# Backward attention loop: operand loads in 28 pieces and result stores issued by SP between the transposing transfers

## The chip, the core and the metric

The kernel runs on one core of a Trainium2 chip. The metric is the device time of one execution in microseconds (us). The core has five engines that this text names: PE (matrix products), DVE (elementwise work on two operands), ACT (functions and copies), POOL (elementwise work, and an issuer of transfers through a software queue) and SP (which only issues transfers, through a hardware queue). All transfers run on the core's 16 DMA engines. Matmuls read SBUF and write PSUM; DMA moves data between SBUF and HBM, and can transpose two-byte data on its way.

## The reference

A transformer block with adaptive layer norm: attention with 32 heads of 16 columns over 2048 tokens of width 512, then a two-layer MLP with a squared ReLU, each with a modulated layer norm and a gate. The kernel computes the block's output and the gradients of nine inputs for a given output gradient.

```
h = layernorm(x) * (1 + ca) + sa
x = x + ga * attention(h, wqkv, wo)
h = layernorm(x) * (1 + cb) + sb
x = x + gb * (relu(h @ w1 + b1)**2 @ w2 + b2)
out, vjp = jax.vjp(block, ...);  grads = vjp(grad_out)
```

The part that matters here is the backward pass of attention. For each head, with E = exp(scores) and the row factors folded into the operands:

```
dS = E * (dO' V'^T)          # 2048 x 2048 per head, elementwise product
dV = E^T dO'    dK = dS^T Q'    dQ = dS K
```

## The kernel before

The kernel runs in phases: layer norm and projections; a forward loop of attention with the MLP's work woven in; weight gradients (lines 776 to 838); the backward loop of attention (lines 840 to 987); and a last phase (from line 989) that turns dQ, dK and dV into the gradients of `x` and `wqkv`.

The backward loop has 1024 steps. `steps` lists them as (head group, key chunk, query tile, pair): 8 head groups of four heads, 4 key chunks of 512 keys (`kc4`), 16 query tiles of 128 queries (`qt`), 2 pairs of heads (`pr`). A head group is 128 steps, a key chunk of it is 32 steps (`BLK`), and 8 steps form a group (`GRP`) of four query tiles.

In each step PE forms scores (`emit_S`, line 852, one step ahead) into a PSUM tile, ACT takes their exponential into `E_u` (line 856), PE forms dO V^T (`emit_D`, line 864), and DVE multiplies the two into `dS_u` (line 870). PE then adds to `accVK`, which holds dV and dK of the key chunk (`emit_V`, line 906, and `emit_K`, line 914). For dQ, dS has to stand with the keys on the partitions. So after the second pair of a query tile SP issues a transposing transfer of `dS_u` into `dST` (line 876): 128 x 2048 elements for the first three tiles of a group and 128 x 1024 for the fourth, whose other half PE transposes (`emit_T`, line 894) and ACT copies (`emit_C`, line 898). `emit_Q` (line 935) multiplies `dST` with K, ten to seventeen steps after the group's first step; ACT copies the result out, and POOL adds it into `dQacc` (line 948) or, in the last key chunk, into `dQstage` (line 953).

`dS_u` has five buffers, one for each two steps, so a buffer is written again ten steps later, and only when its transposing transfer and PE have read it. `dST` has three buffers, one per group.

Two kinds of plain transfers run beside this, all issued by POOL. The operands of the next head group are loaded by `load_one`, nineteen loads, one each five steps from step 32 of a head group on: sixteen of 17 rows of 2048 elements (`iq`, `ik`, `ido`, `iv`, four heads each, 68 KB, line 771) and three of 128 x 2048 elements (`sdo`, `sq`, `sk`, 512 KB, line 767). The tiles have two copies, one per parity of the head group. The results are stored by `put_rows` (line 884): when a head group's dV and dK are copied into `dVKstage`, eight stores of 16 rows of 2048 elements, and when its dQ is complete, four more from `dQstage`. In the last head group the stores are made by pieces of 512 columns, as soon as each is ready, 48 in all. The last phase reads them back from `dT_st` into `dqT` (line 998).

The order of instructions on an engine is the order of the program, loosened by a scheduler; `chain` ties instructions of one queue into a fixed order, here PE's matmuls, and POOL's transfers and sums. SP's transposing transfers are not chained before. Each transfer issued by SP waits until the one eight places before it in SP's queue has landed, since they share eight completion counters; POOL's queue has eight of its own.

Of the kernel before, what the change touches and what calls it, by code (L numbers as in the profile page):

```python
# [17 lines left out]
BF = dt.bfloat16  # L18
F32 = dt.float32

P = 128
# [3 lines left out]
DH = 16  # L25
HG = 8
# [7 lines left out]
def kernel(  # L34
# [8 lines left out]
    TT = n // P  # L43
    QC = n // 512
# [10 lines left out]
    POOL = nc.gpsimd  # L55
    SP = nc.sync
# [34 lines left out]
    def issue_order(later, earlier):  # L91
        tc.add_manual_dep(later.ins, earlier.ins.name, order_only, reason="issue order on one engine")
# [7 lines left out]
    qp_st = dram.tile([HG, P, TT, P], BF, name="qp_st")  # L100
    kp_st = dram.tile([HG, P, TT, P], BF, name="kp_st")
    dop_st = dram.tile([HG, P, TT, P], BF, name="dop_st")
# [7 lines left out]
    dT_st = dram.tile([3, D, n], BF, name="dT_st")  # L110
# [82 lines left out]
    with ExitStack() as ph:  # L193
# [20 lines left out]
        for ic in range(DC):  # L214
            for t in range(3):
                src = wqkv_nat[:, ic, t * 512:(t + 1) * 512].rearrange("p (hg h d) -> p hg h d", hg=HG, h=4)
# [13 lines left out]
        for t in range(TT):  # L230
            for which in range(3):
# [4 lines left out]
                if which < 2:  # L236
                    pad = tokpad[which][t % 2]
                    c0 = DH if which == 0 else 0
# [7 lines left out]
                    else:  # L246
# [3 lines left out]
                                 in_=pad[:])  # L250
# [54 lines left out]
    with ExitStack() as ph:  # L305
# [19 lines left out]
        def chain(key, x):  # L325
            if key in last:
                issue_order(x, last[key])
            last[key] = x

        def pe(mm):  # L330
            chain("pe", mm)
# [236 lines left out]
        with ExitStack() as pa_:  # L568
# [50 lines left out]
            def emit_S(u):  # L619
                qc, hg, kt = units[u]  # L620
                kt_sb, qt_sb, _ = loads[u // TT]
                pair_ps = (sbank[0], sbank[1 + u % 2])
                ET_t[u] = fe.tile([P, 4, 512], BF, name="ET", tag="ET")
                for hq in range(4):
                    r = 32 * hq
                    pe(PE.matmul(pair_ps[hq // 2][:, hq % 2, :], kt_sb[r:r + 32, kt * P:(kt + 1) * P],  # L626
                                 qt_sb[r:r + 32, :], start=True, stop=True, tile_position=(r, 0)))
                for pair in range(2):
                    ACT.activation(ET_t[u][:, 2 * pair:2 * pair + 2, :], pair_ps[pair][:], AF.Exp, scale=SCALE)  # L629
# [108 lines left out]
    strm = tc.alloc_tile_pool(name="phIs", bufs=2, side="right")  # L738
# [5 lines left out]
    steps = [(hg, kc4, qt, pr) for hg in range(HG) for kc4 in range(QC) for qt in range(TT) for pr in range(2)]  # L744
    NS = len(steps)
    BLK = 2 * TT
# [10 lines left out]

    loads = {}
    LOADS = [(nm, src, j) for nm, src in (("iq", QtP), ("ik", KtP), ("ido", dOtP), ("iv", VtP)) for j in range(4)]
    LOADS += [("sdo", dop_st, None), ("sq", qp_st, None), ("sk", kp_st, None)]  # L760

    def load_one(hg, i):
        nm, src, j = LOADS[i]
        L = loads.setdefault(hg, {})
        if j is None:
            L[nm] = strm.tile([P, TT, P], BF, name=nm, tag=nm)
            chain("pool", POOL.dma_start(out=L[nm][:], in_=src[hg]))
        else:
            L[nm] = ops[nm][hg % 2]
            r = 32 * j  # L770
            chain("pool", POOL.dma_start(out=L[nm][r:r + DH + 1, :], in_=src[hg][r:r + DH + 1, :]))

    for i in range(len(LOADS)):
        load_one(0, i)
# [60 lines left out]
    with ExitStack() as ph:  # L835
# [8 lines left out]
        E_t, dS_t, dS_q, dST_t, acc_t = {}, {}, {}, {}, {}  # L844
# [13 lines left out]
        def emit_D(s):  # L858
            hg, kc4, qt, pr = steps[s]
            L = loads[hg]  # L860
            ps = psu.tile([P, 2, 512], F32, name="psD_u", tag="pu")
            for hi in range(2):
                r = 32 * (2 * pr + hi)
                pe(PE.matmul(ps[:, hi, :], L["ido"][r:r + 32, qt * P:(qt + 1) * P],  # L864
                             L["iv"][r:r + 32, kc4 * 512:(kc4 + 1) * 512],
                             start=True, stop=True, tile_position=(r, 0)))
            if pr == 0:
                dS_q[s // 2] = ework.tile([P, 4, 512], BF, name="dS_u", tag="dS_u", bufs=5)
            dS_t[s] = dS_q[s // 2][:, 2 * pr:2 * pr + 2, :]
            DVE.tensor_tensor(dS_t[s], ps[:], E_t[s][:], ALU.mult)  # L870
            g = s // GRP
            if s % GRP == 0:
                dST_t[g] = tpool.tile([P, 4, 16, P], BF, name="dST", tag="dST")
            if pr == 1:
                nb = 16 if qt % 4 < 3 else 8
                SP.dma_start(out=dST_t[g][:, qt % 4, 0:nb, :],
                             in_=dS_q[s // 2].rearrange("q h k -> q (h k)")[:, 0:nb * P], transpose=True)

        stage = {}

        def put_rows(st, hg, c0, w, parts):
            for t3, off in parts:
                for hq in range(4):
                    chain("pool", POOL.dma_start(
                        out=dT_st[t3, hg * 64 + hq * DH:hg * 64 + (hq + 1) * DH, c0:c0 + w],
                        in_=st[32 * hq + off:32 * hq + off + DH, c0:c0 + w]))

        def emit_T(g, half):
            if half == 0:
# [12 lines left out]
        def emit_V(s):  # L902
            hg, kc4, qt, pr = steps[s]
            for hi in range(2):
                r = 32 * (2 * pr + hi)
                pe(PE.matmul(accVK[r:r + 32, :], loads[hg]["sdo"][:, qt, r:r + 32], E_t[s][:, hi, :],  # L906
                             start=(qt == 0), stop=False, tile_position=(0, r), skip_group_check=True))
            del E_t[s]
# [18 lines left out]
        def emit_Q(g, kt):  # L927
            hg, kc4, qt, _ = steps[g * GRP]
            L = loads[hg]
            if kt == 0:  # L930
                acc_t[g] = psa.tile([P, 512], F32, name="accQ", tag="pq")
            accQ = acc_t[g]
            for hq in range(4):
                r = 32 * hq
                pe(PE.matmul(accQ[r:r + 32, :], L["sk"][:, kc4 * 4 + kt, r:r + 32],  # L935
                             dST_t[g][:, :, hq * 4 + kt, :],
                             start=(kt == 0), stop=(kt == 3), tile_position=(0, r), skip_group_check=True))
            if kt == 3:
                del dST_t[g], acc_t[g]
                qc = qt // 4  # L940
                sl = slice(qc * 512, (qc + 1) * 512)
                if kc4 == 0:
                    ACT.activation(dQacc[:, sl], accQ[:], AF.Identity)
                else:
                    part = wk.tile([P, 512], F32, name="dQpart", tag="dQpart")
                    ACT.activation(part[:], accQ[:], AF.Identity)  # L946
                    if kc4 < QC - 1:
                        chain("pool", POOL.tensor_tensor(dQacc[:, sl], part[:], dQacc[:, sl], ALU.add))  # L948
                    else:
                        if qc == 0:  # L950
                            stage["q"] = stg.tile([P, n], BF, name="dQstage", tag="dQstage")
                        st = stage["q"]
                        chain("pool", POOL.tensor_tensor(st[:, sl], part[:], dQacc[:, sl], ALU.add))
                        if hg == HG - 1:
                            put_rows(st, hg, qc * 512, 512, ((0, 0),))
                        elif qc == QC - 1:
                            put_rows(st, hg, 0, n, ((0, 0),))

        emit_S(0)
        for s in range(NS + 12):  # L960
            r = s % (BLK * QC) - BLK
            if s < NS and r >= 0 and r % 5 == 0 and r // 5 < len(LOADS) and steps[s][0] + 1 < HG:
                load_one(steps[s][0] + 1, r // 5)
            if s + 1 < NS:
                emit_S(s + 1)
            if s < NS:
                emit_D(s)
            v = s - 1
            if 0 <= v < NS:
                if v % BLK == 0 and v > 0:  # L970
                    pass
                elif v % BLK == 1 and v > 1:
                    emit_V(v - 1)
                    emit_V(v)
                else:
                    emit_V(v)
            if 0 <= s - 2 < NS:
                emit_K(s - 2)
            g, j = divmod(s - GRP - 2, GRP)
            if 0 <= g < NS // GRP:  # L980
                if 1 <= j <= 2:
                    emit_T(g, j - 1)
                if 1 <= j <= 4:
                    emit_C(g, j - 1)
                for kt in ((0,), (1,), (2, 3))[j - 5] if j >= 5 else ():
                    emit_Q(g, kt)

    strm.release()
    with ExitStack() as ph:
# [6 lines left out]
        for jb in range(12):  # L996
            t3, b = divmod(jb, 4)
# [92 lines left out]
    if _rest_zero:  # L1090
        zt = persist.tile([P, 2048], BF, name="zeros2048")
        DVE.memset(zt[:], 0.0)
        for o in _rest_zero:
# [9 lines left out]
            while r0 < R:  # L1103
                rr = min(P, R - r0)
                c0 = 0
# [35 lines left out]
```

## Time and profile before

| what | value |
|---|---|
| time, median of 3 runs (range) | 2865.84 us (2865.42 to 2877.51) |
| the profiled execution's own time | 2866.86 us |
| its span | 2865.1 us |
| backward loop, first to last `dS_u` multiply | 1363.1 to 2729.9 us |
| PE busy | 2295.4 us (80%) |
| ACT busy | 2256.1 us (79%) |
| DVE busy | 1853.7 us (65%) |
| POOL busy | 579.0 us (20%) |
| hardware queue q1 (SP): packets, share of 16 engines | 1239268, 61.8% |
| software queue q0 (POOL): packets, share of 16 engines | 32704, 12.6% |
| one transposing transfer: issue on SP, from issue to landing (medians) | 1.629 us, 3.9 us |

The span is what the profiler saw of one execution, from the first instruction to the last. The page gives busy times per engine, a chain of waits followed back from the end, groups of instructions by line with what ended the idle time before them, and the transfers by queue. `q1` is the queue that SP feeds, `q0` the one that POOL feeds, `q10` that of ACT. A line such as `L870 DVE ... x1024 | 1218.5, 1221 | 150.1 <-PE psD_u L864 99.5` reads: 1024 instructions of line 870 on DVE, busy 1218.5 us in all, 1221 ns each, DVE idle 150.1 us just before them, 99.5 us of it ended by the matmul of line 864.

### The profile page before, as it was taken

To read this page: it belongs to the slowest core of one execution; us is meant where nothing else is said; L and a number is where in the kernel's file an instruction comes from. 1 tells how busy PE (TensorE), PEld (TensorE's weight loads), DVE (VectorE), ACT (ScalarE), POOL (GpSimd) and SP (SyncE) were. 2 spreads that over 40 slices of the span, in tenths; PEclk is the share of its full clock that TensorE was granted. 3 is DMA by queue.
4 is the path that set the end of the run, shared out by engine and by line. 5 is a ranking of instruction groups with operands and counts; after the bars stand their busy time and mean duration, and the time that the engine had idled before them with its cause. 6 is when DMAs were issued, how large, how long until landed. Compare 5 with 4: busy or idle time off the path is not lost.

```text
span 2865.1 us, 48307 instructions
## 1 busy us (share of the span) xinstructions
PE 2295.4 (80%) x18156; PEld 783.1 (27%) x18261; DVE 1853.7 (65%) x2432; ACT 2256.1 (79%) x2854; POOL 579.0 (20%) x766
## 2 busy tenths in 40 slices
PE   4788879778877875748888888888888888888868
PEld 2323223222322321314222222222222222222223
DVE  5433344425524452743898989989899898989934
ACT  3799999999999995010898989989899898989812
POOL 7311100410230041052012121111212111121221
PEclk8989969878987996969799999999999998999989
DMA  7931245435553544667799999999989999999985
GB/s 200 221 101 62 70 145 122 132 115 116 128 146 87 134 112 138 151 172 233 156 193 202 186 203 194 190 195 189 204 188 199 193 187 196 189 189 188 184 229 132
DMA packets 1275073, 470.61 MB, mean 164 GB/s; under 512 B 1219635, under 2 KB 1244342, under 8 KB 1273046
## 3 DMA queue, kind: packets, MB, share of 16 engines
q1 hardware_dynamic: 1239268, 357.49, 61.8%
q0 software_dynamic: 32704, 105.82, 12.6%
q10 hardware_dynamic: 2866, 4.20, 0.4%
q8 instruction: 144, 2.36, 0.4%
q14 instruction: 91, 0.75, 0.1%
HBM read 118.49 MB, written 72.56 MB: 67 GB/s over the span
## 4 chain that ended last, share of the span: by engine, by line
PE 16%; DVE 16%; ACT 14%; DMA 7%; issue 6%; SPq 1%; POOL 1%; DVEq 0%; ACTq 0%; another core or an unknown queue 0%; POOLq 0%
DVE dS_u L870 13%; ACT E_u L856 12%; PE psD_u L864 4%; DMA dST<-dS_u 4%; PE accVK L906 3%; PE psS_u L852 3%; ACT dST L898 2%; PE dSt L894 1%; PE jb L1071 1%; PE gb L823 1%; PE accQ L935 1%; DMA tT<-ac 1%; DMA out_dram<-dx0t 1%; DMA h2r<-xn_st 1%; DMA out_dram<-woblk 1%
## 5 line engine op out<-in xcount | busy, mean ns | idle before, releaser
L870 DVE TENSOR_TENSOR dS_u<-psD_u,E_u 128x1024 bf16<-128x1024 f32 x1024 | 1218.5, 1221 | 150.1 <-PE psD_u L864 99.5
L856 ACT ACTIVATE E_u<-psS_u 128x1024 bf16<-128x1024 f32 x1024 | 1030.1, 1033 | 88.1 <-PE psS_u L852 57.2
L629 ACT ACTIVATE ET<-sbank 128x1024 bf16<-128x1024 f32 x1024 | 949.1, 1097 | 53.5 <-PE sbank L626 51.6
L864 PE MATMUL psD_u<-iv,ido 32*128 32x512 bf16 x2048 | 415.8, 396 | 169.9 <-ACT E_u L856 154.5
L852 PE MATMUL psS_u<-ik,iq 32*128 32x512 bf16 x2048 | 413.6, 400 | 23.5 <-DVE dS_u L870 19.3
L914 PE MATMUL accVK<-dS_u,sq 128*32 128x512 bf16 x2048 | 419.0, 405 | 0.5 <-DVE dS_u L870 0.5
L906 PE MATMUL accVK<-E_u,sdo 128*32 128x512 bf16 x2048 | 406.8, 406 | 0.0
L626 PE MATMUL sbank<-qt_sb,kt_sb 32*128 32x512 bf16 x2048 | 229.6, 434 | 90.5 <-ACT ET L629 75.2
L636 PE MATMUL oacc<-ET,va 128*32 128x512 bf16 x2048 | 232.3, 442 | 52.0 <-ACT ET L629 46.1
L864 PEld LDWEIGHTS <-ido 32*128 32x128 bf16 x2048 | 163.6, 91 | 355.8 <-issue 352.8
L948 POOL TENSOR_TENSOR dQacc<-dQpart,dQacc 128x512 f32<-128x512 f32 x64 | 80.9, 1264 | 877.5 <-ACT dQpart L946 877.5
L898 ACT ACTIVATE dST<-dSt 128x256 bf16<-128x256 bf16 x512 | 185.7, 391 | 31.3 <-PE dSt L894 30.7
L935 PE MATMUL accQ<-dST,sk 128*32 128x512 bf16 x2048 | 193.6, 398 | 2.7 <-DMA dST<-dS_u 1.7
L852 PEld LDWEIGHTS <-iq 32*128 32x128 bf16 x2048 | 101.5, 91 | 324.6 <-issue 298.4
L906 PEld LDWEIGHTS <-sdo 128*32 128x32 bf16 x2048 | 97.6, 93 | 240.4 <-issue 240.4
L626 PEld LDWEIGHTS <-kt_sb 32*128 32x128 bf16 x2048 | 80.9, 93 | 226.5 <-issue 213.6
L636 PEld LDWEIGHTS <-va 128*32 128x32 bf16 x2048 | 66.1, 95 | 248.9 <-issue 248.6
L733 ACT ACTIVATE dwmod_sb<-dmodbc,silucol 128x2048 bf16<-128x2048 bf16 (+1 forms) x8 | 11.9, 1567 | 153.4 <-DVE dmodbc L712 153.4
L275 PE MATMUL xb<-h1T,wpadT 128*128 128x512 bf16 x338 | 96.4, 396 | 16.9 <-DVE pst L597 8.3
L894 PE MATMUL dSt<-identb,dS_u 128*128 128x128 bf16 x1024 | 105.3, 227 | 1.2 <-ACT dQpart L946 0.7
L642 DVE COPY ostage<-oacc 128x512 f32<-128x512 f32 x32 | 22.0, 687 | 128.6 <-PE oacc L636 128.6
L914 PEld LDWEIGHTS <-sq 128*32 128x32 bf16 x2048 | 99.3, 93 | 8.8 <-issue 8.7
(238 smaller groups left out, 2339.0 us busy)
## 6 DMA issues: line engine op xcount, KB each, us to landing
wbig<-in_B_w_dram POOLq DMA_DIRECT2D x8, 1792.0 KB, 9.5
kt_sb<-KtP SPq DMA_DIRECT2D x24, 512.0 KB, 3.7
va<-va_st SPq DMA_DIRECT2D x32, 336.0 KB, 4.3
dST<-dS_u SPq DMA_TRANSPOSE x512, 3.9
wbig<-w2T_st POOLq DMA_DIRECT2D x4, 1792.0 KB, 13.3
wbig<-w1T_st POOLq DMA_DIRECT2D x4, 1792.0 KB, 8.5
dztok_st<-tokh POOLq DMA_DIRECT2D x8, 896.0 KB, 4.9
dzq<-dztok_st SPq DMA_DIRECT2D x4, 1792.0 KB, 25.7
```

The costliest lines, as they stand in the source:

```text
L626: pe(PE.matmul(pair_ps[hq // 2][:, hq % 2, :], kt_sb[r:r + 32, kt * P:(kt + 1) * P], qt_sb[r:r + 32, :], start=True, stop=True, tile_posit ...
L629: ACT.activation(ET_t[u][:, 2 * pair:2 * pair + 2, :], pair_ps[pair][:], AF.Exp, scale=SCALE)
L636: pe(PE.matmul(oacc[32 * hq:32 * hq + 32, :], lhsT, ET_t[u][:, hq, :], start=(kt == 0), stop=(kt == TT - 1), tile_position=(0, 32 * hq), s ...
L852: pe(PE.matmul(ps[:, hi, :], L["iq"][r:r + 32, qt * P:(qt + 1) * P], L["ik"][r:r + 32, kc4 * 512:(kc4 + 1) * 512], start=True, stop=True, ...
L856: ACT.activation(E_t[s][:], ps[:], AF.Exp, scale=SCALE)
L864: pe(PE.matmul(ps[:, hi, :], L["ido"][r:r + 32, qt * P:(qt + 1) * P], L["iv"][r:r + 32, kc4 * 512:(kc4 + 1) * 512], start=True, stop=True, ...
L870: DVE.tensor_tensor(dS_t[s], ps[:], E_t[s][:], ALU.mult)
L894: pe(PE.transpose(pt[:, j, :], src[:, (8 + j) * P:(9 + j) * P], identb[:]))
L898: ACT.activation(dST_t[g][:, 3, 8 + 2 * j:10 + 2 * j, :], pt[:, 2 * j:2 * j + 2, :], AF.Identity)
L906: pe(PE.matmul(accVK[r:r + 32, :], loads[hg]["sdo"][:, qt, r:r + 32], E_t[s][:, hi, :], start=(qt == 0), stop=False, tile_position=(0, r), ...
L914: pe(PE.matmul(accVK[r:r + 32, :], loads[hg]["sq"][:, qt, r:r + 32], dS_t[s][:, hi, :], start=False, stop=(qt == TT - 1), tile_position=(0 ...
L935: pe(PE.matmul(accQ[r:r + 32, :], L["sk"][:, kc4 * 4 + kt, r:r + 32], dST_t[g][:, :, hq * 4 + kt, :], start=(kt == 0), stop=(kt == 3), til ...
```

## The change

Four things change, all in the backward loop and its loads.

- The three 512 KB loads become four pieces each (128 x 512 elements, 128 KB), so a head group has 28 loads. They are made at every third step from step 22 of the head group before, where it was every fifth from step 32.
- The loads for head groups 1 to 7 are issued by SP. Those for head group 0, ahead of the loop, stay on POOL, also in 28 pieces.
- The stores are no longer issued at once. `put_rows` appends them to a list, and SP issues one at every fourth step; in the last three quarters of the last head group one at every step, and what is left after the loop.
- SP's transposing transfers, loads and stores are chained, so that they keep the order of the program.

```diff
-    LOADS += [("sdo", dop_st, None), ("sq", qp_st, None), ("sk", kp_st, None)]
+    LOADS += [(nm, src, 4 + j) for nm, src in (("sdo", dop_st), ("sq", qp_st), ("sk", kp_st)) for j in range(4)]
+
+    def issue(hg, **kw):
+        if hg == 0:
+            chain("pool", POOL.dma_start(**kw))
+        else:
+            chain("sp", SP.dma_start(**kw))
...
-        if j is None:
-            L[nm] = strm.tile([P, TT, P], BF, name=nm, tag=nm)
-            chain("pool", POOL.dma_start(out=L[nm][:], in_=src[hg]))
+        if j >= 4:
+            if j == 4:
+                L[nm] = strm.tile([P, TT, P], BF, name=nm, tag=nm)
+            ts = slice((j - 4) * TT // 4, (j - 3) * TT // 4)
+            issue(hg, out=L[nm][:, ts, :], in_=src[hg][:, ts, :])
         else:
...
-            chain("pool", POOL.dma_start(out=L[nm][r:r + DH + 1, :], in_=src[hg][r:r + DH + 1, :]))
+            issue(hg, out=L[nm][r:r + DH + 1, :], in_=src[hg][r:r + DH + 1, :])
...
-                SP.dma_start(out=dST_t[g][:, qt % 4, 0:nb, :],
-                             in_=dS_q[s // 2].rearrange("q h k -> q (h k)")[:, 0:nb * P], transpose=True)
+                chain("sp", SP.dma_start(out=dST_t[g][:, qt % 4, 0:nb, :],
+                                         in_=dS_q[s // 2].rearrange("q h k -> q (h k)")[:, 0:nb * P],
+                                         transpose=True))
...
+        rows = []
+
+        def put_row():
+            st, hg, c0, w, t3, off, hq = rows.pop(0)
+            chain("sp", SP.dma_start(
+                out=dT_st[t3, hg * 64 + hq * DH:hg * 64 + (hq + 1) * DH, c0:c0 + w],
+                in_=st[32 * hq + off:32 * hq + off + DH, c0:c0 + w]))
 
         def put_rows(st, hg, c0, w, parts):
             for t3, off in parts:
                 for hq in range(4):
-                    chain("pool", POOL.dma_start(
-                        out=dT_st[t3, hg * 64 + hq * DH:hg * 64 + (hq + 1) * DH, c0:c0 + w],
-                        in_=st[32 * hq + off:32 * hq + off + DH, c0:c0 + w]))
+                    rows.append((st, hg, c0, w, t3, off, hq))
...
-            r = s % (BLK * QC) - BLK
-            if s < NS and r >= 0 and r % 5 == 0 and r // 5 < len(LOADS) and steps[s][0] + 1 < HG:
-                load_one(steps[s][0] + 1, r // 5)
+            r = s % (BLK * QC) - 22
+            if s < NS and r >= 0 and r % 3 == 0 and r // 3 < len(LOADS) and steps[s][0] + 1 < HG:
+                load_one(steps[s][0] + 1, r // 3)
+            if rows and (s % 4 == 1 or s >= NS - BLK * QC + BLK):
+                put_row()
...
+        while rows:
+            put_row()
```

## The prediction

> **What bounds the kernel now.** First the page's groups and chain, then the loop's own waits, then stretches of the loop.
>
> ```profile
> DVE dS_u L870 13%; ACT E_u L856 12%; PE psD_u L864 4%; DMA dST<-dS_u 4%; PE accVK L906 3%; PE psS_u L852 3%; ACT dST L898 2%; PE dSt L894 1%; PE jb L1071 1%; PE gb L823 1%; PE accQ L935 1%; DMA tT<-ac 1%; DMA out_dram<-dx0t 1%; DMA h2r<-xn_st 1%; DMA out_dram<-woblk 1%
> L870 DVE TENSOR_TENSOR dS_u<-psD_u,E_u 128x1024 bf16<-128x1024 f32 x1024 | 1218.5, 1221 | 150.1 <-PE psD_u L864 99.5
> L856 ACT ACTIVATE E_u<-psS_u 128x1024 bf16<-128x1024 f32 x1024 | 1030.1, 1033 | 88.1 <-PE psS_u L852 57.2
> ```
>
> The backward loop takes 1366.8 us of the span (first `dS_u` multiply at 1363.1, last starts at 2728.7 and takes 1.2). One step holds a 1.221 us multiply on DVE; ACT has 1.033 us of `E_u` and 0.20 us of `dST` copies beside it. Where nothing disturbs it, eight steps take 10.35 us (starts of every eighth multiply), 1.294 a step, set by DVE, ACT and PE together. 1024 such steps are 1324.8 us, so 42 us are lost to something. Who waits for the transposing transfers:
>
> ```profile
> L876 SPq DMA_TRANSPOSE dST<-dS_u x512: 1231/1629/7387, 1366.0 to 2729.1; - x171
> its engine sat idle before it (us, times) until:
> who waited for it (us, times):
>   DVE dS_u L870: 23.8, 11
> ...
> DMA to landing us min/median/max: 2.9/3.9/11.2
> ```
>
> DVE waited 23.8 us for them (a `dS_u` buffer still being read). A head group is 128 steps, sixteen blocks of eight; their lengths place the 42 us: 24 in the first four blocks of head groups 1 to 7, 12 in the last four blocks, 2 between, 5 in the loop's first 32 steps, before any store. POOL's order in time shows what is issued there:
>
> ```profile
> 1875.67 3.87 POOL L884 DMA_DIRECT2D dT_st<-dVKstage  x8 [8.34 <-ACT dVKstage L921]
> ...
> 1887.86 1.96 POOL L884 DMA_DIRECT2D dT_st<-dQstage  x4 [0.30 <-POOL dQstage L953]
> 1889.82 2.00 POOL L771 DMA_DIRECT2D iq<-QtP  x4
> ```
>
> Twelve stores and four loads come in bursts; late in a group come the 512 KB `sdo`, `sq`, `sk`. The DMA engines have room, but not much (columns: stretch, PE, PEld, DVE, ACT, POOL, clock, DMA share, GB/s):
>
> ```profile
> 1275.00:1285.00 10.00, 0.00 (x0) 0.10 (x1) 0.00 (x0) 0.00 (x0) 2.94 (x2) 0.50 1.01 423
> 1884.00:1888.00 4.00, 2.51 (x28) 0.85 (x25) 2.84 (x3) 2.90 (x5) 1.41 (x2) 1.00 1.23 277
> 2137.00:2147.40 10.40, 8.88 (x90) 2.80 (x88) 9.55 (x9) 9.44 (x15) 1.73 (x2) 1.00 0.88 191
> ```
>
> Plain loads alone move 423 GB/s, 26.4 per engine. Transposes catching up reach 277 GB/s, so a full one (524 KB) costs each engine 1.89 us; in a quiet stretch 191 GB/s at share 0.88 make it 2.42 us.
>
> **The change, part by part.** PE, ACT and DVE keep their order; all 196 loads for later head groups and all 132 stores leave POOL's queue and stand between the 512 transposes in SP's.
>
> *POOL* loses 16 x 0.52 + 3 x 0.57 + 12 x 0.49 = 16 us of issue per head group. It is busy 31 of 171 us there: worth 0. The first head group's loads stay on POOL, nine more issues of some 0.55 us ahead of the loop, hidden by the weight gradients that run till 1360: 0.
>
> *SP's issue.* 64 transposes x 1.63 = 104 us per head group, plus 40 transfers at 0.43 (the `qt_sb` loads that SP issues) = 17: 121 of 165.6. No bound. Each transfer also waits for the one eight places earlier, about 7.4 steps or 9.6 us in the load stretch, above the usual landing of 3.9. A store that waits for its stage (ACT's 0.59 us copy; POOL's sum, written 28 steps before its turn) holds the next transpose for under a step. All of this lies under the slack: a `dS_u` buffer is wanted eight steps (10.35 us) after its transpose is issued, less 3.9 of landing = 6.4; `accQ` wants `dST` seven steps after, less 2.9 = 6.2. I use 6.3. Without that cover each held us is a us of DVE.
>
> *Stores.* 16 rows of 4 KB: one row per engine, 0.155 us at 26.4 GB/s, one store per four steps. The bursts go: -24 (bounds 0 and -24). Some seven per head group fall into the load stretch and lengthen the queue below by 1.1 us: 7 x 1.1 = +8.
>
> *`sdo`, `sq`, `sk` in quarters:* 131 KB each, 0.31 us per engine; with the transposes (3.5 x 2.1 per eight steps) 8.2 of 10.35 us. Covered: -12 (bounds 0 and -12).
>
> *The sixteen 17-row loads, now one per three steps.* Before shows them only on POOL's queue: the packet records give 17 rows and 31 four-byte packets per load, nine rows starting at once and eight right after, so two rows per engine, 0.31 us. How SP's hardware queue deals 17 rows no row shows: that cost lies between 0.31 us on nine engines and 17 x 4096 B / 26.4 = 2.64 us on one. Its rows that come nearest: every transfer it issues has a multiple of 16 rows, or one row.
>
> ```profile
> q10 hardware_dynamic: 2866, 4.20, 0.4%
> ```
>
> ACT's four hardware transfers hold 512 + 512 + 1792 + 1 data packets; 49 are left, 3 x 16 + 1. So this path posts a completion only for engines that take part, and it was never seen with unequal shares, which POOL's queue makes in its own way (31, not 16). Equal shares of 17 rows are one engine or seventeen. I take one engine as likelier, about 4 to 1.
>
> The Trainium skill ("DMA: Bandwidth & Descriptors", section "Why a DMA increments its semaphore by 16 and not by 1") says it outright: the hardware path uses the largest number up to 16 that divides the outermost sizes, hence one for 17, and POOL's path deals rounded-up shares. The nine-engine records agree with its second half; no run here shows the first.
>
> Then one engine has, over the 48 steps of these loads (62.1 us quiet): 16 x 2.64 = 42.2 us of loads and 21 full-size transposes (24, six of them half) at 2.1, between 1.89 and 2.42, = 44.1: 86.3. Everything behind it on that ring waits; a transpose has landed only when its slowest engine has. 86.3 - 62.1 - 6.3 of slack = 17.9 us per head group, seven times = +125. Lower bound: both kinds at 26.4 GB/s, 42.2 + 21 x 1.24 = 68.2, which the slack just covers: 0. Upper bound: in the forward phase a transpose behind a `kt_sb` load (1.24 us of work) landed 3.96 us after issue against 2.34, 1.3 times the work; 16 x 3.43 + 21 x 2.42 = 105.7, 37.3 each, +261.
>
> *The end.* The last four stores leave POOL at 2743.28 to 2745.2, behind four `dx1t` loads and other stores, and `dqT` follows. On SP they need the last sum (about 2737.7 without POOL's stores) and 4 x 0.43: some 5 us sooner, -5 (0 to -8).
>
> Sum: +125 + 8 - 24 - 12 - 5 = +92. The profiled execution took 2866.86 us (span 2865.1; median of the runs 2865.84, 1 us less): **2959 us**; 2928 with 1.89 us per transpose, 3115 at the upper bound.
>
> **Rivals.**
> 1. *The 17 rows are spread as on POOL.* Then a load costs 0.31 us per engine, bursts and long loads are gone and nothing is added: -24 - 12 - 2 - 5, of which I leave 5 for new small delays: 2866.9 - 38 = 2829. For it: the same transfer spread before. Against: another path issued it.
> 2. *One engine, but bytes alone count.* At 26.4 GB/s for both kinds the slack covers the queue and the stores' gain remains: 2866.9 - 24 - 5 = 2838. It is decided by 1.24 us per transpose; the best stretch shows 1.89, against it.
> 3. *Nothing moves but the issuer.* If a 4 KB packet delays a transpose equally from either queue, delays shift place and the sum is only the tail and POOL's free issue: 2862. Against it, the waits come from bursts, which the change spreads. The Trainium skill (same page, section "Issuing engines are not separate DMA queues") holds that transfers share the 16 engines whoever issues them and that only issue time is saved; the stretch at share 1.23, POOL's packets slowing SP's, agrees with the sharing.
>
> **How the numbers follow.** Forecast 0.75, rival 1 0.14, rival 2 0.05, rival 3 0.06. One engine gets 0.8, as above, less rival 2. The likeliest's own range is 2900 to 3115. For 8 in 10 the range reaches down to rival 1, 2830, and up to 3080, leaving out about 0.07 below and 0.1 above. A measurement of this kernel tells 0.5% (14 us) from no change: faster 0.18 (rivals 1 and 2, most of them), same 0.07 (rival 3 and edges), slower 0.75.
>
> **What would show it.** Right: eight-step blocks of 13 to 16 us from step 24 to 72 of head groups 0 to 6, 10.35 elsewhere; DVE's wait for `dST<-dS_u` at 100 us or more; landings of 17-row loads of 5 us and more; transposes there issuing in 3 us or more; the last head group near 166 us; few stalls in the first 16 steps. Wrong: 17-row loads landing in some 3 us with transposes at 1.6, all head groups near 166 (rival 1), or stalls as before at other places (rival 3). A loop that is long but without waits for `dST<-dS_u` would break the mechanism itself.

## The result, and the profile after

The changed kernel takes 3132.51 us (median of 6 runs, 3126.9 to 3143.74) against 2865.63 us: a ratio of 1.0933, with a 95% interval of 1.0901 to 1.0966. It is slower, as forecast, by almost three times as much (267 us against 92), and outside the range.

The profiled execution took 3143.74 us, 276.9 more than that of before. The backward loop has 271.8 of them (1638.6 us against 1366.8, first to last `dS_u` multiply); it begins 4.0 us later, and what follows it takes 1.1 us longer. The page of the changed kernel, in the lines that answer to those shown before (the numbers of lines have moved by 8 to 14); the last line is the one of before for `accQ`:

```profile
DMA dST<-dS_u 16%; DVE dS_u L878 10%; ACT E_u L864 9%; PE psD_u L872 3%; PE psS_u L860 3%; PE accVK L920 3%; ACT dST L912 2%; PE accQ L949 2%; PE gb L831 1%; PE dSt L908 1%; DMA tT<-ac 1%; DMA out_dram<-dx0t 1%; PE jb L1089 1%; DMA out_dram<-wqblk 1%; DMA out_dram<-woblk 1%
L878 DVE TENSOR_TENSOR dS_u<-psD_u,E_u 128x1024 bf16<-128x1024 f32 x1024 | 1218.9, 1221 | 421.5 <-DMA dST<-dS_u 260.4
L864 ACT ACTIVATE E_u<-psS_u 128x1024 bf16<-128x1024 f32 x1024 | 1032.7, 1031 | 344.6 <-PE psD_u L872 270.1
L949 PE MATMUL accQ<-dST,sk 128*32 128x512 bf16 x2048 | 225.1, 460 | 121.7 <-DMA dST<-dS_u 89.1
```

```profile
L935 PE MATMUL accQ<-dST,sk 128*32 128x512 bf16 x2048 | 193.6, 398 | 2.7 <-DMA dST<-dS_u 1.7
```

The transposing transfers have gone from 4% of the chain to 16%, its first place. The multiplies and exponentials themselves are as they were (1221 ns; 1033 and now 1031 ns); DVE waited 260.4 us for a `dS_u` buffer that a transfer still read, where it was 23.8, and PE another 89.1 us for `dST`, where it was 1.7. The loop's lengths by eight steps (starts of every eighth multiply, in us; one row per head group) show the place:

```
                steps 0 to 31            32 to 63                64 to 95                96 to 127     sum
before, 3  11.93 13.57 10.46 10.29 10.38 10.35 10.42 11.11 10.38 10.35 10.35 10.35 10.38 10.35 10.35 10.36  171.4
after, 0   11.22 12.28 11.73 10.82 19.66 20.38 12.94 20.49 21.12 11.50 10.53 10.35 10.38 10.35 10.35 10.35  214.4
after, 3   10.38 10.35 10.29 10.29 15.28 18.29 19.05 18.26 19.06 13.16 11.80 10.87 10.38 10.35 10.35 10.35  208.5
after, 7   10.38 10.35 10.29 10.29 10.38 10.35 10.29 10.29 10.38 10.35 10.34 10.35 10.38 10.35 10.35 10.38  165.5
```

From head group 1 on, the stalls in the first 32 steps are gone. The sixteen 17-row loads, made at steps 22 to 67, have put larger ones in their place, and head group 7, which loads nothing, runs at the quiet pace throughout. Two stretches within such a stall in head group 1, of 2.4 and 2.5 us (columns as before: PE, PEld, DVE, ACT, POOL, clock, DMA share, GB/s):

```profile
1633.75:1636.15 2.40, 0.00 (x0) 0.00 (x0) 0.00 (x0) 0.00 (x0) 0.00 (x0) 0.50 0.05 20
1636.50:1639.00 2.50, 1.16 (x12) 0.29 (x16) 2.20 (x2) 0.00 (x0) 0.00 (x0) 0.50 1.24 287
```

In the first, no engine of the core computes, and the DMA engines are 0.05 busy: one of sixteen is 0.06. The packet records say which work that is: twelve 4 KB rows of one load, most of them 159 ns long and each starting where the one ahead ends, so on one engine; not one transposing packet starts on any engine, though one was issued at 1633.26. In the second stretch the transposes run again at 287 GB/s. SP's own order around it (start, duration):

```profile
1624.02 0.39 SPq L766 DMA_DIRECT2D iq<-QtP  x1
1624.46 0.31 SPq L893 DMA_DIRECT2D dT_st<-dVKstage  x1
1624.86 5.52 SPq L884 DMA_TRANSPOSE dST<-dS_u  x1
1630.47 0.39 SPq L766 DMA_DIRECT2D iq<-QtP  x1
1630.95 1.23 SPq L884 DMA_TRANSPOSE dST<-dS_u  x1
1632.24 0.93 SPq L893 DMA_DIRECT2D dT_st<-dVKstage  x1
1633.26 4.37 SPq L884 DMA_TRANSPOSE dST<-dS_u  x1
1637.72 0.40 SPq L766 DMA_DIRECT2D ik<-KtP  x1
1638.21 5.42 SPq L884 DMA_TRANSPOSE dST<-dS_u  x1
```

A load takes 0.4 us of SP's time, but the next full-size transpose behind it holds SP for 4.4 to 5.5 us instead of 1.6 (the 1.23 us row is one of half the size). There is hardly a gap between the rows: SP has next to no time left.

### The profile page after: what moved, and what is told of

Read it like the earlier page. It is cut to its first block, busy times and chain, and to the rows that moved or that the text cites. A ratio compares the mean times of both kernels' runs of the same rounds, so it can differ in the third digit from the quotient of the medians.

```text
span 3142.0 us, 48403 instructions
## 1 busy us (share of the span) xinstructions
PE 2405.1 (77%) x18261; PEld 796.3 (25%) x18261; DVE 1853.8 (59%) x2432; ACT 2264.1 (72%) x2854; POOL 453.6 (14%) x510
## 4 chain that ended last, share of the span: by engine, by line
DMA 20%; PE 16%; DVE 12%; ACT 11%; issue 4%; SPq 1%; POOL 0%; DVEq 0%; ACTq 0%; POOLq 0%
DMA dST<-dS_u 16%; DVE dS_u L878 10%; ACT E_u L864 9%; PE psD_u L872 3%; PE psS_u L860 3%; PE accVK L920 3%; ACT dST L912 2%; PE accQ L949 2%; PE gb L831 1%; PE dSt L908 1%; DMA tT<-ac 1%; DMA out_dram<-dx0t 1%; PE jb L1089 1%; DMA out_dram<-wqblk 1%; DMA out_dram<-woblk 1%
## 5 line engine op out<-in xcount | busy, mean ns | idle before, releaser
L878 DVE TENSOR_TENSOR dS_u<-psD_u,E_u 128x1024 bf16<-128x1024 f32 x1024 | 1218.9, 1221 | 421.5 <-DMA dST<-dS_u 260.4
L864 ACT ACTIVATE E_u<-psS_u 128x1024 bf16<-128x1024 f32 x1024 | 1032.7, 1031 | 344.6 <-PE psD_u L872 270.1
L872 PE MATMUL psD_u<-iv,ido 32*128 32x512 bf16 x2048 | 450.8, 430 | 142.1 <-ACT E_u L864 129.1
L860 PE MATMUL psS_u<-ik,iq 32*128 32x512 bf16 x2048 | 449.2, 434 | 116.0 <-DVE dS_u L878 110.5
L928 PE MATMUL accVK<-dS_u,sq 128*32 128x512 bf16 x2048 | 452.4, 438 | 0.5 <-DVE dS_u L878 0.5
L920 PE MATMUL accVK<-E_u,sdo 128*32 128x512 bf16 x2048 | 438.7, 437 | 0.0
L949 PE MATMUL accQ<-dST,sk 128*32 128x512 bf16 x2048 | 225.1, 460 | 121.7 <-DMA dST<-dS_u 89.1
L949 PEld LDWEIGHTS <-sk 128*32 128x32 bf16 x2048 | 59.3, 104 | 155.3 <-issue 80.6
```

What stands on the lines that cost most here:

```text
L860: pe(PE.matmul(ps[:, hi, :], L["iq"][r:r + 32, qt * P:(qt + 1) * P], L["ik"][r:r + 32, kc4 * 512:(kc4 + 1) * 512], start=True, stop=True, ...
L864: ACT.activation(E_t[s][:], ps[:], AF.Exp, scale=SCALE)
L928: pe(PE.matmul(accVK[r:r + 32, :], loads[hg]["sq"][:, qt, r:r + 32], dS_t[s][:, hi, :], start=False, stop=(qt == TT - 1), tile_position=(0 ...
```

## The experiments

**18 rows in place of 17.** The source rows behind the seventeenth are zeros, so one more may be loaded.

```diff
-            issue(hg, out=L[nm][r:r + DH + 1, :], in_=src[hg][r:r + DH + 1, :])
+            issue(hg, out=L[nm][r:r + DH + 2, :], in_=src[hg][r:r + DH + 2, :])
```

> The sixteen loads take 18 rows instead of 17; the added row is a row of zeros, and everything else is as changed. Theory A (a 17-row transfer of SP's queue runs on one DMA engine, and its ring holds the transposes up): 18 rows split evenly over nine engines, two rows each, so the blocks from step 24 to 72 fall from 15 to 20 us to about 10.4 to 11 us, a head group from 210 to about 166 us, and the whole to 2825 to 2850 us. Rival B (any plain transfer that stands in SP's ring between transposes, or the fixed order on SP, holds them up, however its rows are spread): one row more changes nothing, 3130 to 3150 us.

Measured: 2822.31 us in one run. Every head group from 1 on takes 165.4 to 166.4 us. Theory A stands, rival B falls: the same number of transfers in the same order in the same ring, with more bytes, and no stall. The transposes of this kernel, and who waits for them:

```profile
L884 SPq DMA_TRANSPOSE dST<-dS_u x512: 1231/1617/3767, 1365.4 to 2692.6; - x171
its engine sat idle before it (us, times) until:
who waited for it (us, times):
  ACT dST L912: 0.5, 1
```

The longest issue is 3.8 us (7.4 with 17 rows), and DVE waits for none.

The same kernel in six runs, against the kernel before:

> The change with 18 rows in place of 17, timed. Theory A: 0.985 of the kernel before, 2815 to 2830 us.

Measured: 2825.58 us (2816.82 to 2831.72), a ratio of 0.9869 (0.984 to 0.9898). This version is 1.3% faster than the kernel before. Its packet records show the nine engines: the rows of one load start nine at once (1589.58 to 1589.68 us) and nine right behind (1589.76 to 1589.85).

**19 rows.** The same edit with `DH + 3`.

> The same loads with 19 rows (two rows of zeros more). Theory A: 19 rows again share no divisor with 16 engines, so all 19 run on one engine; each load holds it 2 x 0.159 = 0.32 us longer than 17 rows, 16 x 7 x 0.32 = 36 us in all: about 3165 to 3180 us, with the slow blocks still there. Rival B: about 3130 to 3150 us, as with 17 rows and with 18.

Measured: 3147.36 us, with head groups 1 to 6 at 212.7 us on average against 209.8. The slow blocks are there again, so the step from 17 to 18 rows is one of division, not of size: the largest number up to 16 that divides 17 or 19 is one, and for 18 it is nine. The two added rows cost less than half of what was expected, 15 us against 36, which is less than the 17 us over which the runs of the changed kernel spread.

**All loads on POOL.** `issue` sends every load to POOL's queue; stores and transposes stay on SP.

```diff
-        if hg == 0:
+        if True:
             chain("pool", POOL.dma_start(**kw))
```

> All loads go back to POOL's queue, still in 28 pieces at the same steps; stores and transposes stay on SP in their fixed order. Theory A: the loss is gone and the stores' gain stays, head groups of 166 to 169 us, 2835 to 2855 us in all. Rival B in the form that SP's fixed order or the stores cost the time: still above 2950 us.

Measured: 2829.1 us, head groups of 165.5 to 168.4 us. The fixed order on SP and the stores there cost nothing; 17 rows from POOL's queue, two per engine, are harmless.

**Half of the columns.** The 17-row loads with rows of 2 KB; the kernel leaves out the other half of these operands.

```diff
-            issue(hg, out=L[nm][r:r + DH + 1, :], in_=src[hg][r:r + DH + 1, :])
+            issue(hg, out=L[nm][r:r + DH + 1, :n if hg == 0 else n // 2], in_=src[hg][r:r + DH + 1, :n if hg == 0 else n // 2])
```

> The sixteen 17-row loads for head groups 1 to 7 move only half of the columns (2 KB a row instead of 4 KB); the other half of these operands is left out. The profile of the changed kernel has a load holding its engine 4.3 us where 17 rows at 0.159 us would take 2.7. If the extra 1.6 us is a fixed price for each change between transposes and loads on the ring (A1), a load takes 1.35 + 1.6 = 2.95 us, the 48 steps 16 x 2.95 + 21 x 2.07 = 91 us, 22 us over the quiet ones after 6.3 us of slack: head groups of about 188 us, 2975 to 2995 us in all. If the extra grows with the bytes (A2), a load takes 2.15 us, the 48 steps 78 us, 9 us over: head groups of about 175 us, 2885 to 2905 us.

Measured: 2899.71 us, head groups 1 to 6 at 176.8 us on average: A2, the price falls with the bytes, and faster than they do. By the packet records such a load holds its engine 2.16 us (median).

**Loads at every sixth step.** All 17 rows again, but with twice the room.

```diff
-            if s < NS and r >= 0 and r % 3 == 0 and r // 3 < len(LOADS) and steps[s][0] + 1 < HG:
-                load_one(steps[s][0] + 1, r // 3)
+            i = (r // 6 if r % 6 == 0 else 16 + r // 6) if r % 3 == 0 else len(LOADS)
+            if s < NS and r >= 0 and i < (16 if r % 6 == 0 else len(LOADS)) and steps[s][0] + 1 < HG:
+                load_one(steps[s][0] + 1, i)
```

> As changed, with 17 rows, but the sixteen loads stand at every sixth step (from step 22 to 112 of a head group), the quarters between them. The hot engine then has 96 steps, 124.2 us, for 42 full-size transposes at 2.07 us = 87 us and the sixteen loads. If a load holds it 4.3 us wherever it stands (B1), that is 156 us, 25 us over after 6.3 of slack: head groups near 190 us, about 2995 to 3010 us. If the 4.3 us comes only with a ring that is never empty, and a lone load costs its 2.7 us (B2), it is 130 us, which the slack covers: head groups of 166 to 172 us, 2825 to 2870 us.

Measured: 3123.54 us, head groups 1 to 6 at 208.7 us. Neither expectation holds. A load holds its engine 4.62 us here, so B2 is out; but by B1 the room had to bring the head groups from 209.8 to near 190 us, and it takes one us off. The stalls only lie further apart: most blocks from step 32 to 119 take 11 to 19 us.

**Loads from ACT's queue.** The 17-row loads issued by ACT, whose transfers the profile lists under a queue of their own (`q10`), and the same with 18 rows as the measure for it.

```diff
-            issue(hg, out=L[nm][r:r + DH + 1, :], in_=src[hg][r:r + DH + 1, :])
+            if hg == 0:
+                issue(hg, out=L[nm][r:r + DH + 1, :], in_=src[hg][r:r + DH + 1, :])
+            else:
+                ACT.dma_start(out=L[nm][r:r + DH + 1, :], in_=src[hg][r:r + DH + 1, :])
```

> The sixteen 17-row loads for head groups 1 to 7 are issued by ACT, whose hardware queue has rings of its own on the same engines; stores, quarters and transposes stay on SP. By theory A they still run on one engine. If the loss comes from the shared ring (the transposes stand behind the load in SP's ring, and SP stands with them: C1), it is gone, and the time is that of the same kernel with 18 rows on ACT, within 15 us. If it comes from the engine (a transpose needs all sixteen engines at once, and one of them is taken for 2.7 us or more, whoever feeds it: C2), it stays for the most part: 100 to 250 us above the kernel with 18 rows on ACT.

> The same with 18 rows, nine engines: the measure for the run with 17 rows on ACT. ACT issues sixteen loads of some 0.43 us per head group beside its busy 152 of 166 us: 2825 us with 18 rows on SP, and up to 6 x 16 x 0.43 = 41 us more where ACT sets the pace: 2825 to 2866 us.

Measured: 3114.13 us with 17 rows, 2888.51 with 18. The edit moves more than the queue. The loads on ACT are not chained, and the traces show them issued some 25 steps sooner; those for head group 1 stand ahead of the loop, which begins at 1376.2 us with 18 rows (1363.7 with 18 rows on SP) and at 1411.5 with 17. The run with 18 rows is 22 us above its expectation: beside the later start, its head groups 1 to 6 take 174.5 us where they took 166.1. Both runs share this, so their difference still counts: 226 us, of which 35 lie ahead of the loop and 188 in it. That is C2: a transpose is held up by a load in another ring, too. The shared engine is the cause, not the place in SP's queue. The transposes with 17 and with 18 rows on ACT (the first kernel, then the second):

```profile
L887 SPq DMA_TRANSPOSE dST<-dS_u x512: 1231/1634/8491, 1414.4 to 2983.2; - x171
...
  DVE dS_u L881: 148.6, 43
```

```profile
L887 SPq DMA_TRANSPOSE dST<-dS_u x512: 1231/1605/3761, 1379.1 to 2760.4; - x171
...
  DVE dS_u L881: 0.9, 2
```

**The stores, the large loads, and POOL's queue.** Four runs take the gain apart. First, 18 rows on SP with the stores back on POOL in bursts (the `put_rows` of before).

> 18-row loads on SP as in the first run, but the stores go back to POOL in bursts of eight and four. The forecast gave the bursts 24 us and the end of the loop 5: so 24 to 29 us more than with 18 rows and the stores on SP, 2846 to 2851 us, with the lost time in the first four blocks of head groups 1 to 7. If spreading the stores is worth nothing, 2822 us.

Measured: 2829.98 us (2827.46 to 2832.77), 0.9887 (0.9857 to 0.9917) of before. The expectation fails: the loop takes 1331.5 us with bursts from POOL and 1331.6 with stores on SP (18 rows, second profile), and the head groups have no stall at their start. What remains is in the last phase, 133.8 us against 128.4.

Second, 18 rows and stores on SP, but `sdo`, `sq` and `sk` whole (`for j in range(1)` in their list, and the full tile in one transfer).

> 18-row loads and stores on SP, but sdo, sq and sk as one 512 KB load each instead of four quarters. The forecast gave the whole loads on POOL's queue 12 us. If their size was the cause, 8 to 12 us more than with quarters, 2830 to 2834 us, in the blocks around steps 70 to 80; if it was that they came from POOL's queue, no difference, 2822 us.

Measured: 2827.83 us (2823.38 to 2835.44), 0.9882 (0.985 to 0.9914): no difference that the runs can tell from quarters.

Third, everything back on POOL, but in 28 pieces and at the changed steps (both edits above with 17 rows).

> Loads (17 rows, 28 pieces, the changed steps) and stores (in bursts) all back on POOL's queue; of the change only the pieces and steps are left. With the loads alone on POOL the loop had no stalls, and with the stores alone on POOL neither. If it takes both in one queue to stall it (D1), the first blocks of the head groups lose some 3 us each again, 2845 to 2865 us; if the steps and pieces of the loads were what mattered (D2), 2820 to 2835 us.

Measured: 2866.42 us (2855.42 to 2870.41), 1.001 (0.9994 to 1.0025): the time of before, with single blocks of 13 to 19 us near the start of head groups. This is D1, 1 us above its range.

Fourth, the kernel before with its stores alone on SP, spread (`rows`, `put_row` and the chained transposes of the change, and nothing else of it).

> The kernel before with one part of the change alone: its stores on SP, one per four steps; the nineteen loads as before, on POOL, every fifth step from step 32. By the forecast's terms the stores' bursts are worth 24 us and the end of the loop 5, and the whole loads' 12 us stay lost: 2835 to 2842 us. If the loads running ahead in POOL's queue made the stalls, most of them stay: 2850 to 2862 us.

Measured: 2832.67 us (2822.76 to 2841.51), 0.9886 (0.9855 to 0.9918), 2 us below what the forecast's terms gave. So bursts of stores cost the loop nothing when POOL loads nothing, loads from POOL cost next to nothing when it stores nothing, and both in its queue cost some 30 us of stalls. To take either away is enough.

## Why the prediction was right or wrong

**Right: the mechanism and its place.** SP's 17-row loads run on one engine, and the transposes wait. The last head group (165.5 us, forecast near 166), the quiet start of the head groups, DVE's wait of over 100 us and transposes that issue in 3 us or more came as listed. The slow blocks stand at steps 32 to 80, where 24 to 72 were forecast, and most take 15 to 21 us, where 13 to 16 were. The landing of the loads on SP is not in the trace. 17 and 19 rows ran on one engine, 18 on nine. The Trainium skill's rule for the number of engines ("DMA: Bandwidth & Descriptors", section "Why a DMA increments its semaphore by 16 and not by 1"), which no run had shown when it was cited, agrees with all three row counts.

**Right in the sum, wrong in the split: what the rest is worth.** The +8 for stores was a longer queue on the one engine, so without that engine the terms are -24 - 12 - 5 = -41. The version with 18 rows, which has everything but the one engine, is at 0.9869, which of 2865.63 us is -37.5 (-29 to -46). Rival 1, the same thing, was put at 2829; 0.9869 of 2865.63 is 2828. But that the sum came out is luck. The terms were priced one by one from where the stalls stood, and they do not add: stores in bursts cost the loop nothing once the loads leave POOL, and the size of the large loads has no price that the runs can tell.

**Wrong: the size of the one engine's term, +125 us.** From 18 to 17 rows the two ratios give (1.0933 - 0.9869) x 2865.63 = 305 us, 43.6 per head group with loads, where the forecast had 17.9 (19 with the stores' +8). The step that failed is "16 x 2.64 = 42.2 us of loads", and with it the room that the sum gave them: in the runs a load costs the loop 43.6 / 16 = 2.7 us, where the forecast had 17.9 / 16 = 1.1.

A load does not hold its engine for 2.64 us. By the packet records, from the start of its first row to the end of its last, it is 4.43 us (median of the 76 loads whose 17 rows stand by themselves, without a store's rows among them). Most rows take the 159 ns that 26 GB/s gives; some two rows of a load, mostly its first, take longer, 0.8 us in the median. With 4.43 in its place the forecast's own sum is 16 x 4.43 + 44.1 - 62.1 - 6.3 = 46.6 us per head group, near what was measured. The upper bound took 3.43 from a transpose behind a `kt_sb` load with its eight rows per engine, and was too low as well. (Its 3115 is not its sum, either: +261 + 8 - 24 - 12 - 5 on 2866.9 is 3095.)

That agreement is in part luck. While a load's first rows run, packets of the transpose ahead still start, for 0.8 us and some 500 packets of 256 bytes in the median, a quarter of a full transpose, which the 44.1 counts as well. And the sum fails with loads at every sixth step: 16 x 4.62 + 42 x 2.1 - 124.2 - 6.3 = 32 us, measured 208.7 - 165.5 = 43.2. For each of the runs with one engine, a load's hold, counted in the same way, and its cost (head groups 1 to 6 above 165.5 us, by sixteen):

| loads | holds its engine | costs the loop | difference |
|---|---|---|---|
| 17 rows, half of the columns | 2.16 us | 0.71 us | 1.45 us |
| 17 rows, every third step | 4.43 us | 2.77 us | 1.66 us |
| 19 rows, every third step | 4.68 us | 2.95 us | 1.73 us |
| 17 rows, every sixth step | 4.62 us | 2.70 us | 1.92 us |

A load costs what it holds less some 1.4 to 1.9 us, and twice the room adds only 0.3 to that. So one engine did not have the room that the forecast gave it, 62.1 - 44.1 = 18 us per 48 steps. What the room is stays open. One candidate is SP's issue, of which the forecast said "No bound": it added the issues at 1.63 us and found 121 of 165.6 us. In head groups 1 to 6, SP is free for 16% of the 48 steps with 18 rows (its issues sum to 52.2 of 62.0 us), and for 4% with 17 rows, because the next transpose behind a load holds it for 4.7 us on average instead of 1.7. SP's spare time of some 10 us and the slack of 6.3 make 1.0 us per load, and 1.6 with twice the room, where the table has 1.7 and 1.9. That fits roughly, but SP may be held only because the transposes stand, and no run changed its time by itself.

**Rivals.** Rival 1 (17 rows spread as on POOL) is out: on SP they run one behind the other. Rival 2 (bytes alone, covered by slack) is out: the transposes do not share the time with a load, they stand. Rival 3 (only the issuer moves) is out: the same 17-row loads, with the stores on SP, take 2829 us from POOL's queue, 3132 from SP's and 3114 from ACT's.

**Open.** Why some of a load's first rows are several times as long as the others is not known. Why loads and stores stall the loop only when both are in POOL's queue is shown as a fact and not explained.

## What to carry to other kernels

Before a transfer is moved from POOL's queue to SP's or ACT's, look at its number of rows: if, as with the 17 and 19 here, no number from 2 to 16 divides it, it may run on one engine, and one more row of padding can be worth a tenth of the time (3132.5 against 2825.6 us here). Add up how long each issue holds its queue, with the engines it must wait for, and not the issue's usual duration alone. Where two kinds of transfers share a queue and a stall, take one of them away before pricing both.

## What the runs showed of the hardware

While one engine works off a plain load, no transposing packet starts on the other fifteen (share 0.05, 20 GB/s, in the stretch above). That stretch is no exception: of the 76 loads counted above, 74 have 1.5 us or more without such a packet, 3.5 us in the median. With loads from ACT's queue the transposes stand in the same way (from 1627.25 to 1629.25 us, for one) or creep, at 49 GB/s here instead of 287:

```profile
1634.00:1636.00 2.00, 1.23 (x10) 0.40 (x13) 1.23 (x2) 0.00 (x0) 0.00 (x0) 0.50 1.34 49
```

This was not in the forecast, which let the other engines run ahead. Whether the fifteen wait for the one, or what feeds all of them waits, no run tells.

PE's granted clock falls over the stalls: 1.00 in the quiet blocks, and 0.68 over a stretch of stalls.

```profile
1575.80:1617.00 41.20, 35.42 (x354) 11.13 (x352) 37.90 (x33) 37.95 (x53) 2.53 (x2) 1.00 0.99 179
1617.00:1682.00 65.00, 44.16 (x358) 12.17 (x356) 38.25 (x33) 38.55 (x53) 2.53 (x2) 0.68 1.22 123
```

The two stretches hold the same 53 ACT and 33 DVE instructions, in 41.2 and in 65.0 us. Over the whole loop, the same 2048 matmuls of line 872 (864 before) take 430 ns each where they took 396:

```profile
L864 PE MATMUL psD_u<-iv,ido 32*128 32x512 bf16 x2048 | 415.8, 396 | 169.9 <-ACT E_u L856 154.5
L872 PE MATMUL psD_u<-iv,ido 32*128 32x512 bf16 x2048 | 450.8, 430 | 142.1 <-ACT E_u L864 129.1
```

By DVE's waits this cost little of the 271.8 us. Those that end with a transpose grew from 23.8 to 260.4 us; those that end with these matmuls grew from 99.5 to 131.6, and PE's own waits for `dST` can be part of these 32 us. No run changed the clock by itself.
